# Who issues the loads of K, V and wo in an attention stage, and when

## The chip, the cores and the metric

The kernel runs on one core of one Trainium2 chip. TensorE (PE) multiplies matrices, VectorE (DVE), ScalarE (ACT) and GpSimd (POOL) do the elementwise work, and SyncE (SP) issues transfers. Each engine works through its own instructions in order and waits on semaphores for the others. Transfers (DMAs) are issued by SyncE, ScalarE or GpSimd, and 16 DMA engines carry them out. The metric is the device time of one execution in microseconds, and of several executions the median.

## The reference

The reference computes a block and its gradients. With x of 2048 rows by 576 columns:

```python
xn = layernorm(x)
q = (xn @ wq) as 32 heads of 128
p = softmax(q @ k_cache.T * 128**-0.5)         # per head, 2048 x 2048
s = (p @ v_cache) of all heads @ wo
g = silu((sigmoid(xn @ w_gate) * (xn @ w_up)) @ w_down)
out = x + s * g
```

It returns `out` and, by `jax.vjp` with `grad_out`, the gradients of x, k_cache, v_cache, wq, wo, w_gate, w_up and w_down. Inputs and outputs are bf16. k_cache and v_cache have 32 heads of 2048 rows by 128.

## The kernel before, in words

The kernel works in stages. The first (some 460 us) computes the layer norm and the gated unit. The second, the attention stage, goes head by head from about 456 us to 3610 us and makes forward and backward of a head together. The third (from 3610 us on) makes the remaining products over all heads. The change lies in the second stage alone.

**A head.** Rows are taken in 16 tiles of 128. Names that occur in the profile:

- `Kn`, `Vn`: K and V of the head as they lie in memory, 16 tiles of 128 rows; partition p holds rows 16 p to 16 p + 15, so that 512 KB come as 4 KB per partition. `KT`, `VT`: their transposes, made by TensorE (line 485) eight tiles at a time: the call for g = 0 reads the first eight tiles and that for g = 1 the rest.
- `QT`, `dOT`: the projections of the normalized input by wq and of the incoming gradient by wo (line 478); `Qn`, `dOn` their transposes.
- `sp` (line 521), `sneg` (523), `Pq` (533): scores, their scaled negative with the running minimum, and the exponentials, which ScalarE makes. `dp` (554), `t` (560), `dSq` (557, 564): the gradient of the scores.
- `PT`, `dST`: transposes of `Pq` and `dSq`, two tiles in one DMA transpose. SyncE issues them (line 568), eight of each per head. They land in four buffers.
- line 597 (`row_mm`): PT times Vn, and dST times Kn. These are the readers that wait for a transpose to land. Line 621 (`kv_mm`): the gradients of K and V, stored by GpSimd as `dkT_d` and `dvT_d`.

**What sets the order.** The attention stage's order on TensorE, VectorE and ScalarE is written out by hand. A head has 64 positions (`HEAD`). `at(pos, fn, ...)` puts a piece of work at a position, `anchor` does so for the scores; all pieces are sorted by position and emitted in that order, and each of the three engines takes its instructions in the order of emission. SyncE and GpSimd aren't in that list (`MAN`): the compiler's scheduler orders what is theirs. Head h begins at b = 64 h, and `back(x)` is position x of the head before, so work that prepares head h stands among that of head h - 1.

**Positions that matter here.** The products of PT and Vn end at position 47.5 of their own head; those of dST and Kn end at position 15.5 of the following head. Transposes of K for the next head stand at 37.2 and 40.0 (`KT_AT`), those of V at 0.2 and 10.4 of its own head (`VT_AT`), that is 64.2 and 74.4 counted from the head before. `prep_wo`, which reads `wo_h`, stands at 52.2 (`WOT_AT`). The projections of the next head's Q, which read `wq_h`, end at 60.2 and the few steps after it.

**Buffers.** `Vn` and `wo_h` have one buffer each; `Kn` has two, used in turn (`ldK`, `ldK2`). `wq_h` has one.

**Loads before.** At `back(20.0)` stands `load_w`: wq in two transfers, a clearing of the padding and wo_h (lines 449 to 454). At `back(35.1)` stands `load_kv`: K in one transfer of 512 KB (line 425) and V in one (line 438). All are GpSimd's, so the position is only the order of emission: the scheduler places them, and they are issued when GpSimd gets to them and the buffer is free. Head 0 loads K and V in halves already (line 419), through GpSimd. In the last head ScalarE issues fifteen loads of wo for the third stage (`load_wo`, line 401).

Of the kernel before, what the change touches and what calls it, by code (L numbers as in the profile page):

```python
# [14 lines left out]
P = 128  # L15
# [81 lines left out]
def kernel(  # L97
# [6 lines left out]
    nc = tc.nc  # L104
# [6 lines left out]
    NT = S // P  # L111
# [78 lines left out]
    wo_h = pk.tile([P, D], bf, name="wo_h")  # L190
# [192 lines left out]
    def at(pos, fn, *args):  # L383
        prog.append((pos, len(prog), fn, args))

    def anchor(pos, fn, *args):
        anchors.append((pos, len(anchors), fn, args))
# [25 lines left out]
            self.PT = [None] * NT  # L413
            self.dST = [None] * NT

    def load_part(dst, src, k):
        for k_ in range(2) if k is None else (k,):
            ts = slice(k_ * NT // 2, (k_ + 1) * NT // 2)
            nc.gpsimd.dma_start(dst[:, ts, :], src.rearrange("(p t) d -> p t d", t=NT)[:, ts, :])

    def load_k(hs, k=None):
        if not k:
            hs.Kn = (late["ldK2"] if hs.h % 2 else ldK).tile([P, NT, P], bf, name="Kn")
        if k is None:
            nc.gpsimd.dma_start(hs.Kn[:], A_k_cache[0, hs.h].rearrange("(p t) d -> p t d", t=NT))
        else:
            load_part(hs.Kn, A_k_cache[0, hs.h], k)

    def load_v(hs, k=None):
        if not k:  # L430
            hs.Vn = ld1.tile([P, NT, P], bf, name="Vn")
            hs.rs_all = hstat.tile([P, NT], f32, name="rs_all")
            hs.rinv_all = hstat.tile([P, NT], f32, name="rinv_all")
            hs.delta = hstat.tile([P, NT], f32, name="delta")
            hs.negdelta = hstat.tile([P, NT], f32, name="negdelta")
            hs.rsc = hstat.tile([P, NT], f32, name="rsc")
        if k is None:
            nc.gpsimd.dma_start(hs.Vn[:], A_v_cache[0, hs.h].rearrange("(p t) d -> p t d", t=NT))
        else:
            load_part(hs.Vn, A_v_cache[0, hs.h], k)  # L440

    def load_kv(hs):
        load_k(hs)
        load_v(hs)

    def load_wq(hs):
        hc = slice(hs.h * P, (hs.h + 1) * P)
        hs.wq = wh.tile([P, DT, P], bf, name="wq_h", bufs=1)
        nc.gpsimd.dma_start(hs.wq[:, :DL, :], A_wq[:DL * P, hc].rearrange("(t p) c -> p t c", p=P))
        nc.gpsimd.dma_start(hs.wq[:KL, DL, :], A_wq[DL * P:, hc])  # L450
        nc.gpsimd.memset(hs.wq[KL:, DL, :], 0.0)

    def load_wo_h(hs):
        nc.gpsimd.dma_start(wo_h[:], A_wo[hs.h * P:(hs.h + 1) * P, :])

    def load_w(hs):
        load_wq(hs)
        load_wo_h(hs)

    def prep_wo(hs, eng):  # L460
        hs.woT = wh.tile([P, DT, P], bf, name="woT_h", bufs=1)
# [140 lines left out]
    def rows(pos, hs, T, rhs, g, sinks, w):  # L602
        bx = Box()
        sink, after = sinks
        for j in range(GQ):
            for kt in range(NT):
                at(pos + w * (j * NT + kt) / (GQ * NT - 1), row_mm, bx, hs, T, rhs, g * GQ + j, kt, sink)
        if after:
            at(pos + w + (DELTA1 if g == 1 else AFTER), after)
# [33 lines left out]
    def o_sink(hs, g):  # L643
        gs = slice(g * GQ, (g + 1) * GQ)
        bx = Box()

        def sink(acc):
            bx.ou = late["wt"].tile([P, GQ, P], bf, name="ou", bufs=1)
            alt.copy(bx.ou[:], acc[:], eng=OUE)
            bx.prod = late["wt"].tile([P, GQ, P], f32, name="prod", bufs=1)  # L650
            nc.gpsimd.tensor_tensor(bx.prod[:], bx.ou[:], hs.dOn[:, gs, :], op=ALU.mult)

        def after():
            prod, ou = bx.prod, bx.ou
            o_n = late["stg"].tile([P, GQ, P], bf, name="o_n", bufs=1)
            nc.vector.tensor_reduce(hs.delta[:, gs], prod[:], axis=AX.X, op=ALU.add)
            nc.gpsimd.tensor_scalar(hs.negdelta[:, gs], hs.delta[:, gs], -1.0, None, op0=ALU.mult)
            nc.gpsimd.tensor_tensor(o_n[:], ou[:], bcast(hs.rinv_all[:, gs], GQ), op=ALU.mult)
            nc.gpsimd.dma_start(on2_d[g * CH:(g + 1) * CH, hs.h * P:(hs.h + 1) * P].rearrange("(t p) d -> p t d", p=P), o_n[:])

        return sink, after

    def dq_sink(hs, g):
        gs = slice(g * GQ, (g + 1) * GQ)

        def sink(acc):
            dq_n = late["stg"].tile([P, GQ, P], bf, name="dq_n", tag="stg", bufs=3)
            nc.vector.tensor_tensor(dq_n[:], acc[:], bcast(hs.rsc[:, gs], GQ), op=ALU.mult)
            nc.gpsimd.dma_start(dq2_d[g * CH:(g + 1) * CH, hs.h * P:(hs.h + 1) * P].rearrange("(t p) d -> p t d", p=P), dq_n[:])

        return sink, None
# [117 lines left out]
    HEAD = 2 * H1  # L789
    XR, ROW_W, ROW_W2, DELTA1 = 16.8, 6.7, 6.15, 5.7  # L790
    KVE, OUE = ("vs", "ss"), "s"
    WOT_AT = 52.2
    QT_AT, DOT_AT = ((32.6, 47.2, 55.2, 60.2), "s"), ((2.2, 6.2, 14.2, 18.2), "s")
    KT_AT, DON_AT, VT_AT, QN_AT = (37.2, 40.0, "s"), (8.9, 22.0, "v"), (0.2, 10.4, "s"), (24.2, 28.2, "s")
    PSTEP, QS_AT = 0.4, (24.5, 43.3)
# [7 lines left out]
    def adds(pos, w):  # L803
        load_[int(pos * FINE) % (HEAD * FINE)] += w
# [3 lines left out]
    for j in range(DT):  # L808
        adds(WOT_AT, 1)
    for p_ in KT_AT[:2] + DON_AT[:2] + VT_AT[:2] + QN_AT[:2]:  # L810
# [54 lines left out]
    for h in range(H):  # L865
        hs = Head(h) if h else first
        b = h * HEAD
        back = lambda x: b - HEAD + x
        if h:
            at(back(20.0), load_w, hs)  # L870
            at(back(35.1), load_kv, hs)
        for c in range(NCH):
            for i in range(DT):
                if h:
                    at(back(QT_AT[0][c] + PSTEP * i), proj, hs, "QT", c, i, QT_AT[1])
                at(b + (DOT_AT[0] if h else DOT_0)[c] + PSTEP * i, proj, hs, "dOT", c, i, DOT_AT[1])
        if h:
            at(back(WOT_AT), prep_wo, hs, "s")
        for g in range(2):
            if h:  # L880
                at(back(KT_AT[g]), prep_kt, hs, g, KT_AT[2])
            at(b + (DON_AT if h else DON_0)[g], prep_don, hs, g, DON_AT[2])
            at(b + (VT_AT if h else VT_0)[g], prep_vt, hs, g, VT_AT[2])
            at(b + QN_AT[g], prep_qn, hs, g, QN_AT[2])
            at(b + QS_AT[g], q_scale, hs, g)
        for p in range(NT // 2):
            at(b + 4 * p + 2 + RINV_AT, s_rinv, hs, p)
            at(b + max(4 * p + 2.1 + RINV_AT, DON_AT[p // 4] + 0.5), s_scale, hs, p)
        for qt in range(NT):
            p1, p2 = b + 2 * qt, b + H1 + 2 * qt  # L890
            for hf in range(NHF):
                anchor(p1 + hf, s_half, hs, qt, hf)
                anchor(p2 + hf, dp_half, hs, qt, hf)
            at(p1 + EXP_AT, s_exp, hs, qt)
            if qt % 2:
                if h == H - 1 and qt - 1 in P_PE:
                    for i, p_ in enumerate(P_PE[qt - 1]):
                        at(b + p_, pe_pair, hs.PT, hs.Pp, qt - 1, "PT", 8, ps_tr, "tr", i, "s")
                else:
                    at(p1 + PT_AT if h else max(p1 + PT_AT, LATE_AT + 0.1), trans_P, hs, qt - 1)  # L900
                if h == H - 1 and qt - 1 in DS_PE:
                    for i, p_ in enumerate(DS_PE[qt - 1]):
                        if len(DS_PE[qt - 1]) == 4:
                            at(b + p_, pe_pair, hs.dST, hs.dSp, qt - 1, "dST", 8, ps_tr, "tr", i, "s")
                        else:
                            at(b + p_, pe_pair, hs.dST, hs.dSp, qt - 1, "dST", NT, late["ps_big"], "big", i, "sv"[i])
                else:
                    at(p2 + DST_AT, trans_dS, hs, qt - 1)
            if qt not in STT2:
                at(p2 + DSM_AT, ds_mul, hs, qt)  # L910
        for g in range(NG):
            rows(b + 8 * g + XR + (0 if h or g else O0), hs, hs.PT, "Vn", g, o_sink(hs, g), ROW_W - (0 if h or g else O0))
            rows(b + H1 + 8 * g + XR, hs, hs.dST, "Kn", g, dq_sink(hs, g), ROW_W2 if g == 2 else ROW_W)
        for half, (pv, pk_) in enumerate(((VA, KA), (VB, KB))):
            kv(b, pv, hs, hs.P, "dOn", half, dvT_d, out_3)
            kv(b, pk_, hs, hs.dS, "Qn", half, dkT_d, out_2)
# [18 lines left out]
    if True:  # L935
# [84 lines left out]
        with tc.tile_pool(name="b1o", bufs=2, reuse_waits="tile") as outp, tc.tile_pool(name="b1t", bufs=3, reuse_waits="tile") as tmpp, \  # L1020
# [17 lines left out]
            class halves:  # L1038
                n, t = 0, None
# [298 lines left out]
```

## Time and profile before

| | us |
|---|---|
| runs (median; lowest to highest) | 4999.9; 4982.95 to 5007.65 |
| the profiled execution | 4992.16 |
| its span | 4990.4 |

How to read a profile. A row of the timeline is: start in us from the span's start, duration in us, engine, line, operation, what it writes `<-` what it reads, shapes, and how many; in brackets the idle time of the engine before it and what ended that. `q` behind an engine's name means that its sequencer issued the instruction (a transfer). A row on waits is: engine and line that waited, what released it, us in total, how often, the longest. A row of a tile or a line gives durations in ns as min/median/max, and the first and last start in us. A row on a DMA queue gives packets, MB and the time its packets took as a share of 16 engines' time; q0 is GpSimd's queue, q1 SyncE's and q10 ScalarE's. In a row of stretches stand the stretch, its length, and the busy time of PE, PE's weight loads, DVE, ACT and POOL with their instructions, then the granted share of TensorE's clock, the DMA share and GB/s. TensorE's clock was granted at 0.997 over the execution.

### The profile page before, as it was taken

To read this page: it belongs to the slowest core of one execution; us is meant where nothing else is said; L and a number is where in the kernel's file an instruction comes from. 1 tells how busy PE (TensorE), PEld (TensorE's weight loads), DVE (VectorE), ACT (ScalarE), POOL (GpSimd) and SP (SyncE) were. 2 spreads that over 40 slices of the span, in tenths; PEclk is the share of its full clock that TensorE was granted. 3 is DMA by queue.
4 is the path that set the end of the run, shared out by engine and by line. 5 is a ranking of instruction groups with operands and counts; after the bars stand their busy time and mean duration, and the time that the engine had idled before them with its cause. 6 is when DMAs were issued, how large, how long until landed. Compare 5 with 4: busy or idle time off the path is not lost.

```text
span 4990.4 us, 103082 instructions
## 1 busy us (share of the span) xinstructions
PE 4886.3 (98%) x43022; PEld 3079.7 (62%) x43760; DVE 3072.9 (62%) x4844; ACT 2475.2 (50%) x3135; POOL 1543.3 (31%) x2206
## 2 busy tenths in 40 slices
PE   9999999999999999999999999999999999999999
PEld 3445776666666666666666666666657777655554
DVE  6545878888887888888787887887632222110111
ACT  5534666766666676676666666766502222100000
POOL 4323333333343333334333333333323332211000
PEclk9999999999999999999999999999999999999999
DMA  7887999999999999999999999999999989999898
GB/s 258 279 221 153 206 206 209 209 213 207 206 214 213 210 208 207 206 208 207 209 211 202 210 209 202 206 209 204 224 202 258 248 230 249 279 271 240 185 229 196
DMA packets 2879845, 1086.91 MB, mean 218 GB/s; under 512 B 2685360, under 2 KB 2808240, under 8 KB 2879376
## 3 DMA queue, kind: packets, MB, share of 16 engines
q1 hardware_dynamic: 2789728, 789.32, 87.9%
q0 software_dynamic: 85440, 286.38, 20.1%
q8 instruction: 342, 5.60, 0.5%
q10 hardware_dynamic: 4208, 4.57, 0.4%
q14 instruction: 127, 1.04, 0.1%
HBM read 172.54 MB, written 231.41 MB: 81 GB/s over the span
## 4 chain that ended last, share of the span: by engine, by line
PE 81%; DMA 8%; issue 1%; DVE 0%; ACT 0%; POOL 0%; DVEq 0%; ACTq 0%; POOLq 0%
PE acc L597 18%; PE acckv L621 14%; PE sp L521 8%; PE acc L1266 8%; PE dp L554 7%; DMA dST<-dSq 5%; PE accw L1119 5%; PE accp L478 5%; PE accd L1093 3%; PE dh L1065 2%; PE acc L1185 2%; PE acc L1001 2%; PE acct L485 2%; PE accq L1196 2%; PE acckv L618 2%
## 5 line engine op out<-in xcount | busy, mean ns | idle before, releaser
L533 ACT ACTIVATE Pq<-sneg,nm 128x2048 bf16<-128x2048 bf16 x512 | 1025.7, 2003 | 227.4 <-DVE sneg L523 190.1
L597 PE MATMUL acc<-Kn,dST 128*128 128x128 bf16 x8192 | 937.8, 220 | 39.0 <-DMA dST<-dSq 23.9
L557 DVE SCALAR_TENSOR_TENSOR dSq<-dp,delta,Pq 128x1024 bf16<-128x1024 f32 x544 | 694.7, 1282 | 374.8 <-PE dp L554 371.9
L597 PEld LDWEIGHTS <-dST 128*128 128x128 bf16 x8192 | 669.5, 98 | 397.0 <-DMA dST<-dSq 32.8
L597 PE MATMUL acc<-Vn,PT 128*128 128x128 bf16 x8192 | 899.1, 219 | 13.2 <-DMA PT<-Pq 2.7
L597 PEld LDWEIGHTS <-PT 128*128 128x128 bf16 x8192 | 652.0, 98 | 348.5 <-DMA PT<-Pq 5.1
L560 ACT ACTIVATE t<-dp,negdelta 128x1024 bf16<-128x1024 f32 x480 | 535.1, 1115 | 487.5 <-PE dp L554 477.6
L523 DVE TENSOR_SCALAR_CACHE_REDUCE sneg<-sp,nm 128x1024 bf16<-128x1024 f32 x512 | 656.5, 1282 | 114.8 <-PE sp L521 98.7
L523 DVE TENSOR_SCALAR_CACHE_REDUCE sneg<-sp 128x1024 bf16<-128x1024 f32 x512 | 625.2, 1221 | 98.6 <-PE sp L521 54.1
L554 PE MATMUL dp<-VT,dOT 128*128 128x512 bf16 x1988 | 597.9, 380 | 3.0 <-DVE dSq L557 0.3
L521 PE MATMUL sp<-KT,QT 128*128 128x512 bf16 x1960 | 590.7, 379 | 3.4 <-DVE sneg L523 2.8
L621 PE MATMUL acckv<-dSq,Qn 128*128 128x512 bf16 x1739 | 587.9, 380 | 0.4 <-ACT kv L41 0.3
L621 PE MATMUL acckv<-Pq,dOn 128*128 128x512 bf16 x1681 | 553.5, 379 | 1.7 <-POOL dOn L541 0.3
L564 DVE TENSOR_TENSOR dSq<-t,Pq 128x1024 bf16<-128x1024 bf16 x480 | 377.6, 787 | 0.0
L541 POOL TENSOR_TENSOR dOn<-dOn,rinv_all 128x256 bf16<-128x256 bf16 x256 | 157.1, 614 | 368.3 <-DVE rinv_all L537 317.2
L1119 PEld LDWEIGHTS <-xn_all 128*128 128x128 bf16 x2304 | 224.2, 98 | 28.1 <-DMA xn_all<-xn_d 0.4
L1282 DVE SCALAR_TENSOR_TENSOR junk<-dxn,xn_all 128x576 f32<-128x576 f32 x16 | 12.1, 758 | 362.5 <-ACT dxn L1277 362.5
L1266 PEld LDWEIGHTS <-cf 128*128 128x128 bf16 x2304 | 145.5, 98 | 136.8 <-DMA wqT<-in_A_wq_dram 0.2
L521 PEld LDWEIGHTS <-QT 128*128 128x128 bf16 x2048 | 169.7, 98 | 95.9 <-issue 6.1
L554 PEld LDWEIGHTS <-dOT 128*128 128x128 bf16 x2048 | 169.9, 98 | 95.2 <-issue 5.8
L478 PE MATMUL accp<-xnT,wq_h 128*128 128x512 bf16 x612 | 220.4, 381 | 0.1
L1277 ACT ACTIVATE dxn<-acc 128x512 f32<-128x512 f32 (+1 forms) x32 | 12.8, 406 | 394.9 <-issue 302.1
(217 smaller groups left out, 7272.4 us busy)
## 6 DMA issues: line engine op xcount, KB each, us to landing
h_d<-h_row POOLq DMA_DIRECT2D x48, 384.0 KB, 2.7
a_d<-a_row POOLq DMA_DIRECT2D x48, 384.0 KB, 3.5
b_d<-b_row POOLq DMA_DIRECT2D x48, 384.0 KB, 4.5
a_blk<-a_d SPq DMA_DIRECT2D x18, 1024.0 KB, 6.4
b_blk<-b_d SPq DMA_DIRECT2D x18, 1024.0 KB, 21.8
out_dram<-turn SPq DMA_DIRECT2D x35, 512.0 KB, 4.0
h_blk<-h_d POOLq DMA_DIRECT2D x17, 1024.0 KB, 15.9
on_d<-o_n POOLq DMA_DIRECT2D x128, 128.0 KB, 6.4
```

The lines of the kernel that those rows point to most:

```text
L478: nc.tensor.matmul(acc[:], lhsT=w[:, i, :], rhs=(srcT if i < DL else xnT)[:, i, cs], start=(i == 0), stop=(i == DL))
L521: nc.tensor.matmul(sp[:, c * CH:(c + 1) * CH], lhsT=hs.QT[:, qs], rhs=hs.KT[:, hf * HW_ + c * CH: hf * HW_ + (c + 1) * CH], start=True, st ...
L523: nc.vector.tensor_scalar(sneg[:, hf * HW_:(hf + 1) * HW_], sp[:], -SCALE, None if hf == 0 else nm[:, hf - 1:hf], op0=ALU.mult, op1=ALU.mi ...
L533: nc.scalar.activation(Pq, sneg[:], AF.Exp, bias=nm[:, hf:hf + 1], scale=-1.0, accum_out=hs.rs_all[:, qt:qt + 1])
L554: nc.tensor.matmul(dp[:, c * CH:(c + 1) * CH], lhsT=hs.dOT[:, qs], rhs=hs.VT[:, hf * HW_ + c * CH: hf * HW_ + (c + 1) * CH], start=True, s ...
L557: nc.vector.scalar_tensor_tensor(dSq[:, hsl], dp[:], hs.delta[:, qt:qt + 1], Pq[:, hsl], op0=ALU.subtract, op1=ALU.mult)
L560: nc.scalar.activation(t[:], dp[:], AF.Identity, bias=hs.negdelta[:, qt:qt + 1], scale=1.0)
L564: nc.vector.tensor_tensor(hs.dS[qt][:, hsl], t[:], hs.P[qt][:, hsl], op=ALU.mult)
L597: nc.tensor.matmul(bx.acc[:, j, :], lhsT=T[qt][:, kt, :], rhs=getattr(hs, rhs)[:, kt, :], start=(kt == 0), stop=(kt == NT - 1))
L621: nc.tensor.matmul(bx.acc[i][:], lhsT=w, rhs=slabs[qt][:, k0:k0 + CH], start=(qt == 0), stop=(qt == NT - 1))
L1119: nc.tensor.matmul(acc[:kd, :FB], lhsT=xn_all[:, st, d0:d0 + kd], rhs=blk_[:, st, :], start=(st == 0), stop=(st == NT - 1))
L1266: nc.tensor.matmul(accs[sl][j][:, :nn], lhsT=ch[:, kk, sl * P:(sl + 1) * P], rhs=w_[:, n0:n0 + nn], start=(pi == 0 and kk == 0), stop=(las ...
```

## The change

K and V of heads 1 to 31 are loaded in two halves of 256 KB each (eight tiles of every partition's sixteen), and wo_h is loaded at a place of its own. ScalarE issues these five transfers: K at positions 18.3 and 26.3 of the head before, wo_h at 30.3, V at 50.3 and 60.3. Since ScalarE's order is the written one, each is issued when ScalarE reaches that place, and ScalarE waits there if the buffer isn't free. wq stays with GpSimd at position 20.0. Head 0 loads as before.

```diff
-    def load_part(dst, src, k):
-        for k_ in range(2) if k is None else (k,):
+    def load_part(dst, src, k, eng=nc.gpsimd):
+        for k_ in (k,):
             ts = slice(k_ * NT // 2, (k_ + 1) * NT // 2)
-            nc.gpsimd.dma_start(dst[:, ts, :], src.rearrange("(p t) d -> p t d", t=NT)[:, ts, :])
+            eng.dma_start(dst[:, ts, :], src.rearrange("(p t) d -> p t d", t=NT)[:, ts, :])
...
-    def load_k(hs, k=None):
+    def load_k(hs, k, eng=nc.gpsimd):
         if not k:
             hs.Kn = (late["ldK2"] if hs.h % 2 else ldK).tile([P, NT, P], bf, name="Kn")
-        if k is None:
-            nc.gpsimd.dma_start(hs.Kn[:], A_k_cache[0, hs.h].rearrange("(p t) d -> p t d", t=NT))
-        else:
-            load_part(hs.Kn, A_k_cache[0, hs.h], k)
+        load_part(hs.Kn, A_k_cache[0, hs.h], k, eng)
...
-    def load_wo_h(hs):
-        nc.gpsimd.dma_start(wo_h[:], A_wo[hs.h * P:(hs.h + 1) * P, :])
+    def load_wo_h(hs, eng=nc.gpsimd):
+        eng.dma_start(wo_h[:], A_wo[hs.h * P:(hs.h + 1) * P, :])
...
-    WOT_AT = 52.2
+    WOT_AT, WOH_AT, KN_AT, VN_AT = 52.2, 30.3, (18.3, 26.3), (50.3, 60.3)
...
         if h:
-            at(back(20.0), load_w, hs)
-            at(back(35.1), load_kv, hs)
+            at(back(20.0), load_wq, hs)
+            at(back(WOH_AT), load_wo_h, hs, nc.scalar)
+            for k in range(2):
+                at(back(KN_AT[k]), load_k, hs, k, nc.scalar)
+                at(back(VN_AT[k]), load_v, hs, k, nc.scalar)
```

`load_v` changes as `load_k` does; `load_kv` and `load_w`, which called the loads together, are gone.

More of the change, by code (lines that the diff above doesn't have):

```diff
@@ L414, in __init__, with load_v @@
             self.dST = [None] * NT
-    def load_part(dst, src, k):
-        for k_ in range(2) if k is None else (k,):
+    def load_part(dst, src, k, eng=nc.gpsimd):
+        for k_ in (k,):
             ts = slice(k_ * NT // 2, (k_ + 1) * NT // 2)
-            nc.gpsimd.dma_start(dst[:, ts, :], src.rearrange("(p t) d -> p t d", t=NT)[:, ts, :])
-    def load_k(hs, k=None):
+            eng.dma_start(dst[:, ts, :], src.rearrange("(p t) d -> p t d", t=NT)[:, ts, :])
+    def load_k(hs, k, eng=nc.gpsimd):
         if not k:
             hs.Kn = (late["ldK2"] if hs.h % 2 else ldK).tile([P, NT, P], bf, name="Kn")
-        if k is None:
-            nc.gpsimd.dma_start(hs.Kn[:], A_k_cache[0, hs.h].rearrange("(p t) d -> p t d", t=NT))
-        else:
-            load_part(hs.Kn, A_k_cache[0, hs.h], k)
-    def load_v(hs, k=None):
+        load_part(hs.Kn, A_k_cache[0, hs.h], k, eng)
+    def load_v(hs, k, eng=nc.gpsimd):
         if not k:
@@ L436, in load_v @@
             hs.rsc = hstat.tile([P, NT], f32, name="rsc")
[L437 to L444, printed above, removed]
+        load_part(hs.Vn, A_v_cache[0, hs.h], k, eng)
     def load_wq(hs):
@@ L451, in load_wq @@
         nc.gpsimd.memset(hs.wq[KL:, DL, :], 0.0)
-    def load_wo_h(hs):
[L454 to L458, printed above, removed]
+    def load_wo_h(hs, eng=nc.gpsimd):
+        eng.dma_start(wo_h[:], A_wo[hs.h * P:(hs.h + 1) * P, :])
     def prep_wo(hs, eng):
```

## The prediction, made before the changed kernel had run

> **What bounds the kernel now.** I read the page first, then TensorE's waits, then the DMA queue's own timeline, then the places where TensorE waits. The page says how little there is to win: TensorE is counted busy nearly all the time.
>
> ```profile
> span 4990.4 us, 103082 instructions
> PE 4886.3 (98%) x43022; PEld 3079.7 (62%) x43760; DVE 3072.9 (62%) x4844; ACT 2475.2 (50%) x3135; POOL 1543.3 (31%) x2206
> ```
>
> The change touches only the attention stage, heads 1 to 31. The length of one undisturbed head is read from an instruction that comes once per head at the same place, GpSimd's second scaling of Qn (timeline of GpSimd); the mean head from the first and last issue of the V loads (the tile Vn).
>
> ```profile
> 1484.76 1.90 POOL L511 TENSOR_TENSOR Qn<-Qn,rsc 128x1024 bf16<-128x1024 bf16 x1
> ...
> 1581.45 1.90 POOL L511 TENSOR_TENSOR Qn<-Qn,rsc 128x1024 bf16<-128x1024 bf16 x1
> ```
> ```profile
> L438 POOL DMA_DIRECT2D Vn<-in_A_v_cache_dram x31: 587/587/590, 525.4 to 3465.5; - x31
> ```
>
> Undisturbed: 1581.45 - 1484.76 = 96.69 us. Mean: (3465.5 - 525.4)/30 = 98.00 us. So 1.31 us per head, 30 x 1.31 = 39 us in all, is what disturbances cost; no rearrangement of loads can win more, since TensorE's own order stays as it is. The waits of TensorE in this stage name the disturbance:
>
> ```profile
> PE acc L597 <- DMA dST<-dSq: 23.9, 20, 3.6
> PE acc L597 <- DMA PT<-Pq: 2.7, 5, 0.8
> ```
>
> TensorE waits for DMA transposes, nearly only for those of dS. SyncE issues them, 16 a head. Its timeline and the groups of line 568 (durations in ns, min/median/max) show a second resource as full as TensorE:
>
> ```profile
> 1488.57 47.95 SPq L568 DMA_TRANSPOSE dST<-dSq  x8
> 1536.63 48.14 SPq L568 DMA_TRANSPOSE PT<-Pq  x8
> 1584.87 6.59 SPq L568 DMA_TRANSPOSE dST<-dSq  x1
> ```
> ```profile
> L568 SPq EVENT_SEMAPHORE  x517: 17/28/3541, 464.9 to 3584.6; - x173
> L568 SPq DMA_TRANSPOSE PT<-Pq x255: 4478/5691/10785, 464.9 to 3541.2; - x128
> L568 SPq DMA_TRANSPOSE dST<-dSq x254: 4801/5890/12525, 513.8 to 3584.7; - x127
> ```
>
> In this head 16 transposes take 47.95 + 48.14 = 96.09 us, and SyncE's waits are 28 ns in the median: when a transpose is issued its data was ready before. The transpose queue has 0.6 us a head to spare at best and is behind on average. A transpose takes 4.5 to 4.8 us at the least and 12.5 us at the most. A bad head shows what stretches it:
>
> ```profile
> 2671.84 0.59 POOL L438 DMA_DIRECT2D Vn<-in_A_v_cache_dram  x1 [4.21 <-PE acc L597]
> ...
> 2679.36 0.59 POOL L454 DMA_DIRECT2D wo_h<-in_A_wo_dram  x1
> 2680.23 0.54 POOL L637 DMA_DIRECT2D dvT_d<-kv  x1 [0.28 <-DVE kv L43]
> 2681.25 0.54 POOL L637 DMA_DIRECT2D dvT_d<-kv  x1 [0.48 <-ACT kv L41]
> ...
> 2697.66 0.76 POOL L449 DMA_DIRECT2D wq_h<-in_A_wq_dram  x1 [12.02 <-PE accp L478]
> ```
> ```profile
> 2678.18 12.53 SPq L568 DMA_TRANSPOSE dST<-dSq  x1
> ```
> ```profile
> 2678.18 16.55 DMA dST<-dSq
> ```
>
> V (512 KB), wo_h (144 KB) and two stores (256 KB) are issued within 10 us. The transpose among them takes 12.53 us, and the chain of work runs through it for 16.55 us, to its landing.
>
> **The change, part by part.** A position is 96.69/64 = 1.511 us.
>
> *Transfers moved past GpSimd's queue.* Per head GpSimd loses three issues (K, V, wo_h) and their waits for buffers:
>
> ```profile
> L425 POOL DMA_DIRECT2D Kn<-in_A_k_cache_dram x31: 581/586/588, 465.1 to 3417.4; - x31
> ```
> ```profile
> L454 POOL DMA_DIRECT2D wo_h<-in_A_wo_dram x32: 549/590/592, 351.6 to 3369.8; - x32
> ```
> ```profile
> POOL wq_h L449 <- PE accp L478: 235.5, 29, 13.4
> POOL Vn L438 <- PE acc L597: 127.9, 30, 4.9
> POOL Kn L425 <- PE accp L478: 64.0, 30, 2.2
> ```
>
> That is 0.586 + 0.587 + 0.590 = 1.76 us of issue and (127.9 + 64.0)/30 = 6.4 us of waiting per head. I count both at nothing: TensorE's waits above name no store or load of GpSimd's. Late next on that queue is the wait for the wq_h buffer, which stays.
>
> *ScalarE's issues.* Five transfers a head (four of 256 KB, one of 144 KB). ScalarE already issues such loads in the last head:
>
> ```profile
> L401 ACTq DMA_DIRECT2D xnT<-in_A_wo_dram x8: 374/374/422, 3490.0 to 3534.6; - x8
> L401 ACTq DMA_DIRECT2D dsT<-in_A_wo_dram x7: 374/374/415, 3540.3 to 3576.4; - x7
> ...
> DMA to landing us min/median/max: 4.0/6.1/8.9
> ```
> ```profile
> 3502.44 2.00 ACT L533 ACTIVATE Pq<-sneg,nm 128x2048 bf16<-128x2048 bf16 x1
> 3502.45 0.37 ACTq L401 DMA_DIRECT2D xnT<-in_A_wo_dram  x1
> ```
> ```profile
> 1433.60:1530.30 96.70, 95.82 (x864) 61.48 (x879) 79.57 (x117) 65.44 (x74) 34.74 (x47) 1.00 1.17 212
> ```
>
> Cost 5 x 0.374 = 1.87 us a head. The issue at 3502.45 runs under the exponential begun at 3502.44, and ScalarE (fourth of the five busy times) works 65.44 of 96.70 us, so I price it at 0. Without that cover it would be 30 x 1.87 = 56 us.
>
> *Waits that ScalarE now makes.* Behind a wait stand the exponentials and copies, and TensorE behind these. K's old readers end at position 15.5 and K is loaded at 18.3, behind the exponential of 18.1, which needs scores of 17; V's end at 47.5 and it is loaded from 50.3, behind the copy `t` of position 50. TensorE has passed those readers by then: 0. If not, V's wait would be GpSimd's: 127.9/30 = 4.3 us a head.
>
> *Are the halves in time?* K: 18.3 and 26.3 against transposes at 37.2 and 40.0, 28.6 and 20.7 us. V: 50.3 and 60.3 against 64.2 and 74.4, 21.0 and 21.3 us. The slowest landing above is 8.9 us: 0. This needs a reader to wait for its own half alone; if the first V transpose waited for both, it would have 3.9 positions = 5.9 us, under the median landing of 6.1. At the start of the kernel x_all comes in parts too, and its first reader began before the second part was issued:
>
> ```profile
> 2.98 0.82 DVE L241 BATCH_NORM_STATS2 stats<-x_all 128x6 f32<-128x288 bf16 x2 [2.12 <-DMA x_all<-in_A_x_dram]
> ```
> ```profile
> 3.07 0.43 SPq L201 DMA_DIRECT2D x_all<-in_A_x_dram  x1
> ```
>
> *What the moved bytes cost the transposes.* This decides. 512 + 512 + 144 KB = 1.20 MB a head change queue. The DMA queues of an ordinary head (1433.6 to 1530.3) and of the last one (3493.3 to 3590), with MB and share of 16 engines:
>
> ```profile
> q1 hardware_dynamic: 66775, 16.97, 104.1%
> q0 software_dynamic: 1184, 3.44, 12.0%
> ```
> ```profile
> q10 hardware_dynamic: 4208, 4.57, 18.6%
> q0 software_dynamic: 768, 2.10, 8.9%
> ```
> ```profile
> 3499.47 48.19 SPq L568 DMA_TRANSPOSE PT<-Pq  x7
> 3547.82 42.25 SPq L568 DMA_TRANSPOSE dST<-dSq  x6
> ```
>
> By SyncE's time: the ordinary head is 8 x 4.478 + 8 x 4.801 = 74.2 us at the shortest; the other 21.9 us come with 3.44 MB of GpSimd's traffic, 6.35 us a MB. The last head's 13 transposes take 90.4 us, 60.2 at the shortest. Of the 30.3 left, 2.10 MB from GpSimd take 13.3; some 4.0 of ScalarE's 4.57 MB fall into the stretch (13 of its 15 loads are issued there) and have 17.0, 4.2 us a MB. That gives 1.20 x (4.2 - 6.35) = -2.6 us a head. Were all 30.3 us ScalarE's, 7.6 us a MB: +1.5 us a head. By packet time: GpSimd 0.120 x 96.7/3.44 = 3.37 us a MB, ScalarE 0.186 x 96.7/4.57 = 3.94 (+0.7 us a head), but beside it in the same head GpSimd 0.089 x 96.7/2.10 = 4.10 (-0.2 us). The ends are -2.6 and +1.5. I take -0.6: the pair from one head is the fairest and says -0.2, and SyncE's time leans the same way, though its 6.35 also holds stores, so most of -2.6 isn't K's and V's.
>
> *Where they lie.* V's burst before the fourth dS transpose is halved and wo_h leaves it (912 KB in 10 us become 512), but V's second half, at 60.3, joins wq_h just after. A queue that never idles does not gain by bytes pushed along it: the dS waits at V go, later ones grow. I take 0.
>
> Sum: 30 x -0.6 = -18 us. The profiled execution took 4992.2 us for its span of 4990.4 and would take 4974; it stands 7.7 us under the median of the runs, 4999.9, so that the predicted median is 4982.
>
> The Trainium skill ("DMA: Bandwidth & Descriptors", "Issuing engines are not separate DMA queues") says that transfers of whichever engine run on the same 16 DMA engines and interleave, so that only issue time is saved; by it the term of -0.6 would be 0 and the time 4999.9. The pair 3.94 against 4.10 agrees to 4%.
>
> **The rivals.** *Only moved:* price equal, the queue as full: 4999.9, within 10 us. For it: 3.94 against 4.10. Against: 4.2 against 6.35.
>
> *All disturbance goes:* with 1.3 us less a head the queue falls below TensorE's 96.69, so 4999.9 - 39 = 4961. For it: the worst transposes lie at V's burst. Against: it also waits for PT (2.7 us), whose transposes are not V's neighbours.
>
> *Slower:* a third queue is dearer to the transposes. ScalarE's halves run beside GpSimd's stores instead of in line with them, in rows of half the length, and the full transpose queue hands each us to TensorE. At 7.6 us a MB: 30 x 1.5 = 45 us, 5045; at the packet price +0.7, 5021. It decides from +0.83 us a head (25 us in all), 52 ns a transpose. For it: no other slack than 0.6 us. Against: the same-head pair. The skill's same page ("Queues, rings and completion order") says that each DMA engine takes turns between the queues that have work; by that the transposes' share falls while both others are filled. No run here shows the shares.
>
> **How the numbers follow.** Half a per cent, 25 us, is what a measurement of this kernel can tell from no change. Forecast 0.45, its own range -8 to -36 us (4964 to 4992): 0.24 of it beyond -25, 0.21 within. All goes 0.16, faster. Only moved 0.14, same. Slower 0.25: 0.22 beyond +25, 0.03 within. Faster 0.40, same 0.38, slower 0.22. The range from 4956 to 5028 leaves out the deepest gains (0.06) and the dearer half of the slower case (0.12).
>
> **What would show it.** Right: transposes of dS with a median under 5.85 us and none near 12.5; TensorE's wait for dST near 10 us instead of 23.9; the mean distance of wq_h loads near 97.4 us; ScalarE's issues at 0.37 us without idle time before them. Wrong: a longer median transpose (slower), the waits as large but moved to the sixth dS transpose (only moved), or TensorE waiting for ScalarE's copies, or for VT behind a late half of V, which I price at nothing.

## The result, and the profile after

The changed kernel takes 4966.8 us in the median (4954.6 to 4985.4 over 13 runs), the kernel before, run beside it, 4987.4 us (4977.2 to 5011.4). The ratio is 0.9955 with a 95% interval of [0.9942, 0.9968]: 0.45% or 22 us faster, just under the half per cent that the prediction set as its border. The profiled execution of the changed kernel, 4954.6 us, is the fastest of its 13, so its profile shows the gain at its largest.

The page of the changed kernel:

```profile
span 4952.9 us, 103882 instructions
...
q0 software_dynamic: 75024, 249.30, 17.1%
q10 hardware_dynamic: 26528, 41.66, 3.6%
```

37.1 MB have moved from GpSimd's queue (q0, 286.4 MB before) to ScalarE's (q10, 4.6 MB before). The bytes in all are the same. What TensorE waited for in the attention stage (480 to 3610 us), longest first:

```profile
PE acc L583 <- DMA PT<-Pq: 3.5, 3, 2.4
...
PE acc L583 <- DMA dST<-dSq: 0.9, 1, 0.9
```

Line 583 is line 597 of the kernel before. The wait for transposes of dS fell from 23.9 to 0.9 us, and that for PT stayed small. The loads of wo_h come once per head and give the mean head:

```profile
L444 ACTq DMA_DIRECT2D wo_h<-in_A_wo_dram x31: 334/334/367, 500.4 to 3409.6; - x31
```

(3409.6 - 500.4)/30 = 96.97 us, against 98.00 before and 96.69 undisturbed: 31 of the 39 us are gone in this execution.

The waits on transposes alone don't add up to that: they were 23.9 + 2.7 = 26.6 us before and are 3.5 + 0.9 = 4.4 us now, 22 us less. TensorE's clock has a part in it. In the execution before it was granted at one half in four stretches of the attention stage, of 3.4, 3.4, 3.4 and 6.8 us, and each lies at one of the four longest waits for dS (2.1 to 3.6 us). Here are one of these waits and the clock in the stretch beside it (third number from the end):

```profile
2392.56 0.23 PE L597 MATMUL acc<-Kn,dST 128*128 128x128 bf16 x1 [2.27 <-DMA dST<-dSq]
```
```profile
2393.20:2396.60 3.40, 3.40 (x17) 1.84 (x16) 1.88 (x2) 0.43 (x1) 0.00 (x0) 0.50 1.24 276
```

From 480 us on to the stage's end the changed kernel has one such stretch, of 3.4 us, at its longest wait (2.4 us, for P). If half of such a stretch is lost, an estimate, they cost 8.5 us before and 1.7 us now; with the waits that makes 29 of the 31 us. Not every long wait has such a stretch: one of 3.7 us in run 10 has none.

SyncE's transposes (line 554, 568 before):

```profile
L554 SPq EVENT_SEMAPHORE  x639: 17/28/4415, 464.6 to 3554.0; - x160
L554 SPq DMA_TRANSPOSE PT<-Pq x255: 4791/5867/10469, 464.7 to 3511.0; - x128
L554 SPq DMA_TRANSPOSE dST<-dSq x254: 4736/5804/7897, 513.1 to 3554.1; - x127
```

The median of the dS transposes hardly moves (5890 to 5804 ns), that of the P transposes even rises (5691 to 5867). What goes is the longest of dS, 12525 to 7897 ns; the longest of P hardly moves (10785 to 10469). The queue is as full as before, also in an undisturbed head:

```profile
2598.36 49.09 SPq L554 DMA_TRANSPOSE PT<-Pq  x8
2647.55 41.71 SPq L554 DMA_TRANSPOSE dST<-dSq  x7
```

ScalarE's issues run under its other work, as in the last head before. Here is the second one of K:

```profile
2629.50 2.00 ACT L519 ACTIVATE Pq<-sneg,nm 128x2048 bf16<-128x2048 bf16 x1
2629.51 0.33 ACTq L419 DMA_DIRECT2D Kn<-in_A_k_cache_dram  x1
```

### The profile page after: what moved, and what is told of

Its sections match the earlier page's. It is cut to its first block, busy times and chain, and to the rows that moved or that the text cites. A ratio compares the mean times of both kernels' runs of the same rounds, so it can differ in the third digit from the quotient of the medians.

```text
span 4952.9 us, 103882 instructions
## 1 busy us (share of the span) xinstructions
PE 4918.6 (99%) x43760; PEld 3078.2 (62%) x43760; DVE 3068.3 (62%) x4844; ACT 2474.3 (50%) x3135; POOL 1500.0 (30%) x2113
## 4 chain that ended last, share of the span: by engine, by line
PE 87%; DMA 2%; issue 1%; DVE 0%; POOL 0%; ACT 0%; DVEq 0%; ACTq 0%; POOLq 0%
PE acc L583 18%; PE acckv L607 16%; PE dp L540 9%; PE sp L507 9%; PE acc L1255 8%; PE accp L464 5%; PE accw L1108 5%; PE accd L1082 3%; PE acc L990 3%; PE dh L1054 2%; PE acc L1174 2%; PE acct L471 2%; PE accq L1185 2%; PE acckv L604 2%; DMA PT<-Pq 1%; PE accl L1118 1%
## 5 line engine op out<-in xcount | busy, mean ns | idle before, releaser
L607 PE MATMUL acckv<-dSq,Qn 128*128 128x512 bf16 x1856 | 628.3, 379 | 0.3 <-ACT kv L41 0.3
L607 PE MATMUL acckv<-Pq,dOn 128*128 128x512 bf16 x1856 | 613.9, 379 | 0.4
L507 PE MATMUL sp<-KT,QT 128*128 128x512 bf16 x2048 | 609.7, 379 | 3.2 <-DVE sneg L509 2.8
L540 PE MATMUL dp<-VT,dOT 128*128 128x512 bf16 x2048 | 609.5, 379 | 1.3 <-DVE dSq L543 0.3
L637 POOL TENSOR_TENSOR prod<-ou,dOn 128x512 f32<-128x512 bf16 x128 | 165.9, 1296 | 245.2 <-ACT ou L41 242.8
L464 PE MATMUL accp<-xnT,wq_h 128*128 128x512 bf16 x640 | 230.5, 380 | 0.0
```

The source lines that it names most:

```text
L464: nc.tensor.matmul(acc[:], lhsT=w[:, i, :], rhs=(srcT if i < DL else xnT)[:, i, cs], start=(i == 0), stop=(i == DL))
L507: nc.tensor.matmul(sp[:, c * CH:(c + 1) * CH], lhsT=hs.QT[:, qs], rhs=hs.KT[:, hf * HW_ + c * CH: hf * HW_ + (c + 1) * CH], start=True, st ...
L540: nc.tensor.matmul(dp[:, c * CH:(c + 1) * CH], lhsT=hs.dOT[:, qs], rhs=hs.VT[:, hf * HW_ + c * CH: hf * HW_ + (c + 1) * CH], start=True, s ...
L607: nc.tensor.matmul(bx.acc[i][:], lhsT=w, rhs=slabs[qt][:, k0:k0 + CH], start=(qt == 0), stop=(qt == NT - 1))
```

## The experiments

Theory A is the prediction's: a MB costs the transposes less when ScalarE issues it than when GpSimd does. Theory B: it is the place, that is, 512 KB of V no longer lie before the fourth transpose of dS. Ratios are to the kernel before on the same chip, with 95% intervals. Diffs are against the changed kernel and show the lines that matter. Waits are those of the one profiled execution of a run.

**1. The engine alone.**

```diff
-            ts = slice(k_ * NT // 2, (k_ + 1) * NT // 2)
+            ts = slice(0, NT) if k_ is None else slice(k_ * NT // 2, (k_ + 1) * NT // 2)
...
-            at(back(WOH_AT), load_wo_h, hs, nc.scalar)
-            for k in range(2):
-                at(back(KN_AT[k]), load_k, hs, k, nc.scalar)
-                at(back(VN_AT[k]), load_v, hs, k, nc.scalar)
+            at(max(back(52.9) - HEAD, 0.0), load_wo_h, hs, nc.scalar)
+            at(back(16.2), load_k, hs, None, nc.scalar)
+            at(back(48.1), load_v, hs, None, nc.scalar)
```

With `None` a load is whole; runs 3, 7 and 8 have the same line for `ts`.

> Only the issuing engine changes: ScalarE issues K and V whole (512 KB each) and wo_h at about the positions at which GpSimd issued them in the profile of before (16.2, 48.1, 52.9). Theory A, the price: a MB that ScalarE issues costs the transposes less than one from GpSimd. It expects most of the gain here: 0.9955 to 0.997 of before, a mean transpose shorter by 0.04 to 0.08 us. Theory B, the place: what counts is that V's burst no longer lies before the fourth dS transpose. It expects 0.999 to 1.001 and TensorE's wait for dST still above 15 us.

Measured 1.0008 [0.9994, 1.0023], with 16.6 us of waiting for dST. Theory A falls: the engine alone is worth nothing.

**2. The halves alone.**

```diff
-            at(back(WOH_AT), load_wo_h, hs, nc.scalar)
-            for k in range(2):
-                at(back(KN_AT[k]), load_k, hs, k, nc.scalar)
-                at(back(VN_AT[k]), load_v, hs, k, nc.scalar)
+            at(back(20.0), load_wo_h, hs)
+            for fn in (load_k, load_v):
+                for k in range(2):
+                    at(back(35.1), fn, hs, k)
```

> Only the halves: GpSimd issues K and V in halves of 256 KB as the buffers come free, both halves one behind the other, and wo_h as before. Theory A (price of the engine) expects no change, 0.999 to 1.001. Theory B (place) expects none either, since the bytes stay where they were. A third, C, that rows of 2 KB in smaller transfers let the transposes through better, expects 0.996 to 0.998.

Measured 1.0032 [1.0017, 1.0047]: slower, which no theory had. TensorE's wait for dST in its profile, the row again in us, times and longest:

```profile
PE acc L583 <- DMA dST<-dSq: 39.4, 29, 4.8
```

**3. The places without the halves.**

```diff
-            for k in range(2):
-                at(back(KN_AT[k]), load_k, hs, k, nc.scalar)
-                at(back(VN_AT[k]), load_v, hs, k, nc.scalar)
+            at(back(KN_AT[0]), load_k, hs, None, nc.scalar)
+            at(back(VN_AT[0]), load_v, hs, None, nc.scalar)
```

> The changed kernel with the halves undone: ScalarE issues K whole at 18.3, V whole at 50.3 and wo_h at 30.3. Theory A expects the gain to stay, 0.9955 to 0.997 of before. Theory B expects half of it or less, 0.997 to 1.000, with TensorE's wait for dST back above 10 us, since 512 KB lie again before the fourth dS transpose.

Measured 1.0030 [1.0006, 1.0054]: the whole gain gone, and more. Its waits, in an execution of 5029.0 us where the median is 5006.2, show two places:

```profile
PE acc L583 <- DMA dST<-dSq: 34.0, 24, 5.2
PE acc L583 <- DMA PT<-Pq: 25.8, 21, 3.5
```

The wait for PT, 2.7 us before, is new: K whole at 18.3 does to the transposes of P what V whole does to those of dS. A head's fourth P transpose takes 7.8 us in the median there, 5.9 before. At 15.9, where GpSimd issued it, it did not (2.7 us), and hardly at 16.1, where ScalarE issued it in run 1 (5.8 us).

**4. wo_h back to GpSimd.**

```diff
-            at(back(WOH_AT), load_wo_h, hs, nc.scalar)
+            at(back(20.0), load_wo_h, hs)
```

> The changed kernel with wo_h (144 KB a head) given back to GpSimd, which issues it as its buffer comes free, about position 52.6, beside V's first half. Theory A expects an eighth of the gain to go: 0.995 to 0.9965. Theory B expects more, as wo_h lies again in the crowded stretch: 0.996 to 0.998, and the fourth dS transpose longer by 0.3 us or more.

Measured 0.9973 [0.9956, 0.9989]. By the medians the 144 KB, an eighth of the bytes, take 0.18 of the 0.45%, as Theory B expected; but the intervals overlap (0.9956 to 0.9968), so the loss isn't clear of noise. Theory B's other sign fails: the fourth dS transposes, 6.7 us in the median of the changed kernel, are at 6.6 us here and not 0.3 us longer. The wait for dST is 9.1 us, 7.2 of it in the 5 us after the following head's first exponential:

```profile
PE acc L583 <- DMA dST<-dSq: 9.1, 8, 1.6
```

**5. GpSimd at the written places.** ScalarE writes an element per partition and tile of each half as a mark, and GpSimd's load has to wait for it.

```diff
-            eng.dma_start(dst[:, ts, :], src.rearrange("(p t) d -> p t d", t=NT)[:, ts, :])
+            if eng is nc.scalar:
+                nc.scalar.copy(dst[:, ts, 0:1], ident[:, 0:NT // 2].unsqueeze(2))
+            nc.gpsimd.dma_start(dst[:, ts, :], src.rearrange("(p t) d -> p t d", t=NT)[:, ts, :])
```

wo_h has the same mark in its first column.

> The changed kernel's halves and places, but GpSimd issues the transfers: ScalarE writes one element per partition and tile into each half (and one column of wo_h) at the written place, and GpSimd's load of that half has to wait for it. The price theory (A) has lost its ground after the first four runs; Theory B, place and size of the transfers whichever engine issues them, expects the changed kernel's gain, 0.994 to 0.997 of before. If ScalarE's queue is needed beside the places (A as a condition), 0.999 to 1.002.

Measured 1.0021 [1.0000, 1.0042]. No gain; but counted from each head's first exponential GpSimd issued the five loads 1.8 to 3.0 us later than ScalarE had in the changed kernel (medians), so place and engine were not yet separate (run 10). The marks are five more copies of some 0.2 us a head on ScalarE; no wait of TensorE names them.

**6. Halves in pairs.**

```diff
-    WOT_AT, WOH_AT, KN_AT, VN_AT = 52.2, 30.3, (18.3, 26.3), (50.3, 60.3)
+    WOT_AT, WOH_AT, KN_AT, VN_AT = 52.2, 30.3, (18.3, 18.4), (50.3, 50.4)
```

> The changed kernel with both halves of K issued at 18.3 and 18.4 and both of V at 50.3 and 50.4: halves, but not apart. Theory B (bytes within the span of one or two transposes) expects what whole transfers at these places gave, 1.001 to 1.006 of before, with waits both for PT near 40 us into a head and for dST near 85 us. Theory C' (size of a transfer: 256 KB let the transposes through, 512 KB don't) expects 0.995 to 0.997.

Measured 1.0007 [0.9985, 1.0029], with 21.0 us of waiting for dST. The halves must lie apart. The pairs are not clearly better than whole transfers: the intervals of 3 and 6 overlap.

**7 and 8. V and wo_h alone; K alone.**

```diff
+            at(back(35.1), load_k, hs, None)
...
-                at(back(KN_AT[k]), load_k, hs, k, nc.scalar)
```
```diff
-            at(back(WOH_AT), load_wo_h, hs, nc.scalar)
+            at(back(20.0), load_wo_h, hs)
...
-                at(back(VN_AT[k]), load_v, hs, k, nc.scalar)
+            at(back(35.1), load_v, hs, None)
```

The first diff, run 7, gives K back to GpSimd, whole; the second, run 8, gives wo_h and V back, V whole.

> V and wo_h as in the changed kernel, K whole by GpSimd as before. Theory B in its simple form, only V's burst before the fourth dS transpose costs time, as the waits of before show no loss near K: 0.995 to 0.997, K's part nothing. If the queue's length is carried from K's burst on to V's place, half of the gain: 0.997 to 0.999.

> K in halves by ScalarE at 18.3 and 26.3, V whole and wo_h by GpSimd as before. Simple Theory B: nothing, 0.999 to 1.001. If the queue's length is carried over from head to head: 0.997 to 0.999.

Measured 1.0005 [0.9986, 1.0024] and 1.0025 [1.0003, 1.0047]. TensorE waits 10.5 and 23.3 us for dST, in run 7 in an execution of 4977.0 us where the median is 4990.1. Theory B in its simple form falls too: V and wo_h, whose place cost nearly all the waiting before, bring nothing clear of noise by themselves, and K, near which nothing waited, makes the difference between 1.0005 and 0.9955. The parts do not add up.

**9. Places 1.2 positions later.**

```diff
-    WOT_AT, WOH_AT, KN_AT, VN_AT = 52.2, 30.3, (18.3, 26.3), (50.3, 60.3)
+    WOT_AT, WOH_AT, KN_AT, VN_AT = 52.2, 31.5, (19.5, 27.5), (51.5, 61.5)
```

> The changed kernel with all five places 1.2 positions (1.8 us) later: K 19.5 and 27.5, wo_h 31.5, V 51.5 and 61.5. In the run in which GpSimd issued the halves at the written places it did so 1.4 to 3.1 us after ScalarE in the changed kernel, and the gain was gone. Theory B (the place alone): this loses the gain too, 0.999 to 1.003, with the waits for dST in the first 6 us of a head that the GpSimd run showed. Theory E (ScalarE's queue is needed beside the places, so that loads don't stand in line with GpSimd's stores): the gain stays, 0.994 to 0.998.

Measured 0.9962 [0.9944, 0.9980], but this was no shift. In the changed kernel V's first half is issued 0.30 us after GpSimd's store of o; in this run as well. The changed kernel, then this run:

```profile
2664.51 0.82 POOL L645 DMA_DIRECT2D on_d<-o_n  x1 [0.29 <-POOL o_n L644]
2664.81 0.34 ACTq L419 DMA_DIRECT2D Vn<-in_A_v_cache_dram  x1
```
```profile
1886.64 0.82 POOL L645 DMA_DIRECT2D on_d<-o_n  x1 [0.29 <-POOL o_n L644]
...
1886.94 0.33 ACTq L419 DMA_DIRECT2D Vn<-in_A_v_cache_dram  x1
```

ScalarE's sequencer issues the load while the instruction ahead of it runs, so a place a little later between the same two instructions changes nothing. Only wo_h moved, by 2.5 us. The run counts as a second measurement of the changed kernel's places: 0.9955 and 0.9962.

**10. GpSimd at the same times.** Run 5 with earlier marks:

```diff
-    WOT_AT, WOH_AT, KN_AT, VN_AT = 52.2, 30.3, (18.3, 26.3), (50.3, 60.3)
+    WOT_AT, WOH_AT, KN_AT, VN_AT = 52.2, 28.5, (16.4, 24.3), (49.0, 59.0)
```

> GpSimd issues the halves behind ScalarE's marks as before, but the marks stand earlier (K 16.4 and 24.3, wo_h 28.5, V 49.0 and 59.0), so that the issues fall within 1 us of those of the changed kernel. Theory B: the gain is back, 0.994 to 0.998 of before. Theory E: no gain, 0.999 to 1.003.

Measured 1.0019 [0.9999, 1.0040]. The waits for dST are back:

```profile
PE acc L587 <- DMA dST<-dSq: 21.3, 17, 3.7
```

Its timeline shows V's halves in one head, with the store of o as in run 9:

```profile
2089.52 0.82 POOL L649 DMA_DIRECT2D on_d<-o_n  x1 [0.29 <-POOL o_n L648]
2090.34 0.56 POOL L421 DMA_DIRECT2D Vn<-in_A_v_cache_dram  x1
...
2103.01 0.54 POOL L421 DMA_DIRECT2D Vn<-in_A_v_cache_dram  x1 [3.11 <-ACT Vn L420]
```

The first half comes 0.82 us after the store instead of 0.30, the second 13.5 us after it. In the changed kernel the second comes 14.8 us after the store of run 9's first fence (2664.51):

```profile
2679.27 0.33 ACTq L419 DMA_DIRECT2D Vn<-in_A_v_cache_dram  x1
```

K's halves, counted as in run 5, come 0.6 us earlier and 1.8 us later than in the changed kernel, wo_h within 0.2 us, V's halves 0.5 us later and 1.3 us earlier. At nearly these times GpSimd's halves bring nothing, and ScalarE's bring 0.45%, or 0.38% in run 9 on the same chip. So the issuing queue seems to matter, but only together with halves and places (run 1 has whole transfers and no effect). It isn't shown beyond doubt: no run excludes what is left of the differences in time.

**11. V's second half later.**

```diff
-    WOT_AT, WOH_AT, KN_AT, VN_AT = 52.2, 30.3, (18.3, 26.3), (50.3, 60.3)
+    WOT_AT, WOH_AT, KN_AT, VN_AT = 52.2, 30.3, (18.3, 26.3), (50.3, 66.3)
```

> The changed kernel with V's second half at 66.3 instead of 60.3, behind wq_h and dq's store instead of just ahead of them, and 12.2 us before its reader. The sixth dS transpose has the least slack left in the changed kernel. If the place is what counts, moving 256 KB away from it gains a little more: 0.993 to 0.996. If only the distance from V's first half counted, as now: 0.9955. Were the half late for its reader, TensorE would wait at the transposes of V at 74.4 and the time go up to 1.000 or more.

Measured 0.9939 [0.9920, 0.9958], 4964.9 us beside 4997.8: the fastest of all variants, though its interval overlaps that of the changed kernel. No wait for a late half appears, and little else is left:

```profile
PE acc L583 <- DMA PT<-Pq: 1.5, 4, 0.6
PE acc L583 <- DMA dST<-dSq: 0.4, 1, 0.4
```

**12. K halved by partitions.** One thing that differs between the halves on the two queues is the length of their packets. Each half's row is 2 KB per partition. ScalarE's queue carries it as packets of 2048 bytes, GpSimd's as packets of 4096. The queues of one head of the changed kernel and of run 5, with packets and MB:

```profile
q10 hardware_dynamic: 720, 1.20, 6.6%
```
```profile
q0 software_dynamic: 1264, 3.62, 15.7%
```

The 720 are 512 of 2048 bytes, 128 of 1152 (wo_h) and 80 that only signal. Run 12 gives K's halves rows of 4 KB on 64 partitions:

```diff
-        load_part(hs.Kn, A_k_cache[0, hs.h], k, eng)
+        if eng is nc.scalar:
+            ps = slice(k * P // 2, (k + 1) * P // 2)
+            eng.dma_start(hs.Kn[ps, :, :], A_k_cache[0, hs.h].rearrange("(p t) d -> p t d", t=NT)[ps, :, :])
...
```

> The changed kernel with K halved by partitions (64 partitions of 4 KB each) instead of by tiles (128 partitions of 2 KB each): same engine, places and bytes. In the traces so far the halves travel in packets of 2048 bytes on ScalarE's queue, but in packets of 4096 bytes on GpSimd's queue, where they gained nothing. Theory F, that the shorter packets are what the gain needs: K's part goes, 0.998 to 1.001 (K whole by GpSimd gave 1.0005). Theory E, that a queue apart from GpSimd's stores and the places are what it needs: the gain stays, 0.994 to 0.997.

Measured 1.0069 [1.0043, 1.0094], the slowest of all. Its page of the queues for one head has 592 packets for the same 1.20 MB, and its waits, in an execution of 5040.0 us where the median is 5017.5, stand at PT, behind K:

```profile
q10 hardware_dynamic: 592, 1.20, 4.0%
```
```profile
PE acc L587 <- DMA PT<-Pq: 37.9, 16, 5.3
PE acc L587 <- DMA dST<-dSq: 18.4, 12, 3.0
```

Theory E (a queue apart from the stores and the places are enough) falls for K in this form. Theory F (short packets) stands, but isn't shown: a transfer to 64 partitions differs in more than the packets' length, and 1.0069 is worse than any whole K.

The runs in one table:

| issued by | transfers | places | ratio |
|---|---|---|---|
| GpSimd | whole | as buffers come free | 1 |
| ScalarE | whole | about the same | 1.0008 |
| ScalarE | whole | written | 1.0030 |
| GpSimd | halves | as buffers come free | 1.0032 |
| GpSimd | halves | written, 1.8 to 3.0 us late | 1.0021 |
| GpSimd | halves | written, within 1.8 us | 1.0019 |
| ScalarE | halves in pairs | written | 1.0007 |
| ScalarE | halves | written (changed kernel; run 9) | 0.9955; 0.9962 |
| ScalarE | halves | V's second at 66.3 | 0.9939 |
| ScalarE, wo_h GpSimd | halves | written | 0.9973 |
| ScalarE, K GpSimd | V halves, K whole | V and wo_h written | 1.0005 |
| ScalarE, V and wo_h GpSimd | K halves, V whole | K written | 1.0025 |
| ScalarE | halves, K's by partitions | written | 1.0069 |

## Why the prediction came out, and where it was wrong

*The number.* Forecast -18 us, measured -20.6 us between the medians and -22 by the ratio. (The forecast time, 4982 us, was 15 us above the measured 4966.8, since it started from a median of three runs, 4999.9, where 13 runs gave 4987.4.) The direction and the size were right, and the sum was not: both of its terms were wrong and made up for each other, so that the number came out by luck.

*"What the moved bytes cost the transposes", the step that decided.* It gave -0.6 us a head to the change of engine. Run 1 changes the engine alone and measures 1.0008, nothing. The step compared the last head's loads by ScalarE with GpSimd's traffic of an ordinary head. But those loads were also short (rows of 1152 bytes) and spread over the head, so the comparison mixed engine, packet length and place, the three things that the experiments had to take apart. The nearer pair, 3.94 against 4.10 us a MB, gave only -0.2 us a head.

*"Where they lie: I take 0."* Wrong: in pairs the halves give 1.0007, apart 0.9955. The argument was that a queue that never idles gains nothing by pushing bytes along it. What it left out is that TensorE loses only through transposes that come later than its reserve, the time between a transpose's landing and the product that reads it. The medians of the transposes after are close to those before, the longest of dS went from 12.5 to 7.9 us, and with it the waiting. The other runs fit: in the profiles of those that gain (the changed kernel, runs 4, 9 and 11) the longest dS transpose took 7.9 to 8.9 us, in the kernel before and all other runs 9.5 to 14.4. That the reserve is the reason is argued from these numbers; no run here measured the reserve itself.

*Right:* the ceiling. 39 us under the profiled execution's 4992.2 is 4953; no execution of any run is below 4954.6. But the rows on waits, on which the prediction put this loss, hold 26.6 of the 39 us; the halved clock beside the longest waits, which it did not look at, has an estimated 8.5 more. Right too that GpSimd's issues and waits (1.76 and 6.4 us a head) were worth nothing (run 1 takes these issues from GpSimd and gains nothing), ScalarE's 0.33 us issues as well, and that a reader waits for its own half alone: with V's second half at 66.3, behind the first V transposes at 64.2, the kernel is the fastest.

*The signs.* The mean distance of the wq_h loads, from head 1's at 446.08 us to the last at 3359.17, came to 97.10 us (97.4 forecast) in the profiled execution, and the median dS transpose to 5.80 (under 5.85), with none near 12.5. TensorE's wait for dST fell to 0.9 us, not to 10. ScalarE's issues took 0.33 us, not 0.37.

*The rivals.* "Only moved" is refuted by 0.9955. "All disturbance goes", -39 us, is nearly what the two profiled executions show (4992.2 to 4954.6, -37.5 us); the medians show 21 to 22 us, a little over half of it. "Slower", by a dearer third queue, did not come: run 1 has the third queue and no loss. But close variants (runs 3, 8 and 12) are slower by 0.25 to 0.7%, where it named 0.4 to 0.9%; runs 3 and 12 differ from the changed kernel only in how the transfers are cut.

*The Trainium skill's rule* that only issue time is saved, whichever engine issues ("DMA: Bandwidth & Descriptors", "Issuing engines are not separate DMA queues"): run 1 agrees (1.0008). For halves at written places it does not seem to hold here: 1.0019 from GpSimd, 0.9955 from ScalarE, at times that differ by up to 1.8 us. The Trainium skill's same page advises against splitting a transfer into halves by partitions, since by it the two serialize ("Rules for kernel authors"); run 12, whose halves lay apart in time, goes further and shows a loss, 1.0069.

*Open:* why halves need ScalarE's queue (packet length, or standing apart from the stores), and why V's and K's parts do not add (1.0005 and 1.0025 alone, 0.9973 for both without wo_h). That a DMA engine changes from one queue to another at the ends of packets, as the Trainium skill has it ("DMA: Bandwidth & Descriptors", "Queues, rings and completion order"), would speak for packet length; no run here shows it.

## What to carry to other kernels

When two resources are both full (here TensorE at 96.69 us a head and the transpose queue at some 96), the same bytes can cost or save half a per cent by how they are cut and where they lie, and the mean durations hardly show it: look at the longest ones and at who waits for them. Cutting a large load into parts that lie apart is worth a trial, but no rule: here it paid only from ScalarE and for K and V together. Before pricing a change of queue from another stage of the same profile, ask what else differs there, and change one thing at a time: of this change, the engine alone, the halves alone, and engine and places without the halves each gave nothing or a loss.

## What the runs showed of the hardware

- The same rows of 2 KB travel in packets of 2048 bytes when ScalarE issues them and of 4096 bytes when GpSimd does (run 5 and the changed kernel, under experiment 12).
- A load by ScalarE is issued while the instruction ahead of it runs; 1.2 positions (1.8 us) later in the written order changed K's and V's times of issue by nothing (run 9).
- In the attention stage of the kernel before, TensorE's clock was granted at one half in stretches of 3.4 or 6.8 us, each beside one of TensorE's four longest waits for transposes (2.1 to 3.6 us). Where they come together, a wait costs more than its own length.
- A transfer of 256 KB to 64 partitions takes ScalarE longer to issue than one to 128: 0.47 against 0.33 us (run 12, K).

```profile
L426 ACTq DMA_DIRECT2D Kn<-in_A_k_cache_dram x62: 472/473/553, 483.4 to 3466.9; - x62
```
